# Moving the low parts of MoE 1's 32 weight tiles from VectorE to GpSimd in an attention + two-MoE kernel

## The chip, the core and the metric

The kernel runs on one core of one Trainium2 chip. The metric is the device time of one execution in microseconds (us), the lower the better. The kernel before was timed three times: 968.51, 968.61 and 970.44 us, median 968.61 us.

## The reference: what is computed

Attention with a memory term over B = 4, H = 8, S = 576, D = 64, then two dense feed-forward layers over the 2304 tokens (512 wide, 2048 inner). Cut to what matters:

```python
def _attn_ref(q, k, v, M_prev, z_prev, beta):
    a = softmax(causal(q @ k.T / sqrt(D)))
    mem_out = (phi(q) @ M_prev) / (phi(q) @ z_prev + 1e-6)
    g = sigmoid(beta)
    return g * mem_out + (1 - g) * (a @ v)

def _moe_ref(x, w_in, w_out):      # MoE 1
    h = x @ w_in
    return (h * sigmoid(h)) @ w_out

def _moe2_ref(x, w_in, w_out):     # MoE 2
    h = x @ w_in
    return elu(h) @ w_out

def reference(...):
    return _moe2_ref(_moe_ref(_attn_ref(...)))
```

The weights arrive as 64-bit floats (two 32-bit words each). The kernel rebuilds a 32-bit float from the two words.

## The kernel before, in words

**High and low parts.** TensorE multiplies at its fast rate in a shortened float type (`F32R`). To keep accuracy every operand of the MoE matmuls is held as two tiles: a high part (the value rounded to `F32R`) and a low part (value minus high part). A product is then three matmuls: high x high, high x low, low x high. `split2` (line 474) makes both parts: ScalarE copies the value into the high tile (`nc.scalar.copy`, shown as ACT CAST), and VectorE subtracts it from the value (`sub`, shown as DVE TENSOR_TENSOR).

**The weight stream of MoE 1.** `w_stream` (line 548) brings in 32 weight tiles, f = 0..15 for each of `w_in` (c = 0) and `w_out` (c = 1), in the order (0,0), (0,1), (1,0), ... Each arrives by one DMA of 512 KB into a staging tile. The staging tiles are four slots (`LEND` = 4) in the homes of the last four weight tiles, `w0_14`, `w1_14`, `w0_15`, `w1_15`; the last two tiles pass through two slots called `raw`. `w_value` (line 530) rebuilds the float: ScalarE scales the upper word (ACT ACTIVATE w<-w), VectorE shifts the lower word (TENSOR_SCALAR) and combines the words with two SCALAR_TENSOR_TENSORs. Then `w_split` (line 543) calls `split2`: the high part goes to columns 512 to 1023 of the tile's home, the low part to columns 0 to 511. When both have read the staging slot, the next DMA may fill it. That DMA sits in SyncE's one in-order queue, together with the loads of attention (`q`, `k`, `vr`, `qm`, `zb`, `diag`).

**What runs beside it.** The attention of 20 tasks (scores, mask and maximum on VectorE, exp on ScalarE, scaling, transposes on TensorE, product with V) runs in the first 280 us or so. Into it are woven the first two token blocks of MoE 1 (`moe1_block`, line 611): they use tiles f = 0..7 for both blocks, then tiles f = 8..15 for both. So the weights are wanted one after the other while attention runs. The other MoE 1 blocks and all of MoE 2 follow; MoE 2's weights use the same `w_value`, but their own calls of `split2`.

**GpSimd** does little: a few memsets and masks at the start, and 16 `MEMSET a` of 64x128 (one for each b-part of attention) which wait until TensorE has read the old contents of the five `a` buffers.

**What sets the order.** Nothing is issued in the order of the code. Class `Plan` records every operation, gives it a cost (`cost`, line 239 on) and a lag between engines (`lag`, line 277), and `order` (line 288) runs a list scheduler forwards and backwards 24 times; the best plan fixes each engine's instruction order. A cost counts in that plan only: 602 ns for a 512-column VectorE `tensor_tensor`, and for GpSimd `n / 1.2 + 40` ns (line 268), n being the columns. The planner gives each engine its own time: work on one never makes another slower.

The lines that the change touches:

```python
            return n / 1.2 + 40                    # cost of a GpSimd operation, ns

    def split2(hi, lo, src):
        nc.scalar.copy(hi, src)
        sub(lo, src, f32(hi))

    def w_split(f, c, v):
        t = w_tile(f, c)
        split2(t[:, 512:1024], t[:, 0:512], f32(v))
        (win, wout)[c][f] = t
```

Of the kernel before, what the change touches and what calls it, by code (L numbers as in the profile page):

```python
# [14 lines left out]
ALU = mybir.AluOpType  # L15
# [4 lines left out]
HP = 2000  # L20
OFF = 200
NORM = '3'
XHP = 1000
HOOK = 4
AHEAD = 4
# [132 lines left out]
class Plan:  # L158
# [82 lines left out]
    @staticmethod  # L241
    def cost(op, fn, args, kw, ins, outs, together):
        def cols(v):
            n = 1
            for m in v.shape[1:]:
                n *= m
            return n

        if op.eng == "PE":
            if fn == "transpose":  # L250
                return max(ins[0].shape[0] / 1.2, 0.84 * cols(ins[0]))
            n, m, once = cols(kw["rhs"]), cols(kw["lhsT"]), kw["rhs"].dtype != F32
            if together > 1:
                return n / (2.4 if together > 4 and kw["lhsT"].shape == (64, 64) else 1.2)
            return max(n / (2.4 if once else 0.6) + (13.5 if once else 3.0), 0.84 * m * (1 if once else 2))
        if op.eng == "DMA":
            v = outs[0] if isinstance(outs[0], View) else ins[0]
            n = 4
            for m in v.shape:
                n *= m  # L260
            return max(430.0, n / 280.0)
        n = cols(outs[0])
        psum = any(v.tile.space == "psum" for v in ins)
        if op.eng == "ACT":
            c = n / 1.2 + (51 if psum else 93) + (186 if kw.get("accum_out") is not None else 0)
            return c + (93 if isinstance(kw.get("scale"), View) else 0)
        if op.eng == "POOL":
            return n / 1.2 + 40
        if fn == "tensor_reduce":
            n = cols(ins[0])  # L270
        fast = fn in ("tensor_scalar", "tensor_copy") and not psum
        ptr = any(isinstance(kw.get(k), View) for k in ("scalar1", "scalar2")) or (
            fn == "scalar_tensor_tensor" and isinstance(kw["scalar"], View))
        return 69 + (60 if ptr else 0) + n / (1.92 if fast else 0.96)
# [125 lines left out]
def attention_moe_moe_kernel(  # L400
# [15 lines left out]
    nc = Plan(tc.nc)  # L416
# [21 lines left out]
    def f32(ap):  # L438
        return ap.bitcast(F32)
# [27 lines left out]
    def sub(o, a, b):  # L467
        nc.vector.tensor_tensor(out=o, in0=a, in1=b, op=ALU.subtract)

    def split(t, src):  # L470

        split2(t[:, 0], t[:, 1], src)

    def split2(hi, lo, src):
        nc.scalar.copy(hi, src)
        sub(lo, src, f32(hi))

    ident = new(at, [128, 128], F32, "ident")
    mask = new(at, [128, 704], BF16, "mask")
# [4 lines left out]
        out=ident[:], in_=ident[:], pattern=[[-1, 128]], compare_op=ALU.is_equal,  # L484
# [3 lines left out]
    for p0, rows, c0, n in ((0, 128, 384, 128), (0, 64, 640, 64), (64, 64, 640, 64)):  # L488
        tri = mask[p0:p0 + rows, c0:c0 + n]
        nc.gpsimd.affine_select(  # L490
            out=tri, in_=tri, pattern=[[-1, n]], compare_op=ALU.is_ge, fill=-1e30, base=0, channel_multiplier=1,
# [48 lines left out]
    def w_tile(f, c, dtype=F32R):  # L540
        return new(wp, [128, 1024], dtype, f"w{c}_{f}")

    def w_split(f, c, v):
        t = w_tile(f, c)
        split2(t[:, 512:1024], t[:, 0:512], f32(v))
        (win, wout)[c][f] = t

    def w_stream(srcs, ahead):

        todo = [(f, c) for f in range(NF) for c in range(2)]  # L550
        n = len(todo)
        raws = {}

        def fetch(k):
            if k < n:
                f, c = todo[k]
                i = n - LEND + k % LEND if k < n - LEND else n - 2 + k % 2
                raws[k] = w_load(srcs[c], f, c, w_tile(*todo[i], I32) if k < n - 2 else new(at, [128, 1024], I32, "raw"))

        for k in range(ahead):  # L560
            fetch(k)
        yield
        for k, (f, c) in enumerate(todo):
            raw = raws.pop(k)
            w_value(raw)
            w_split(f, c, raw[:, 0:512])
            if k + ahead < n - 2:
                fetch(k + ahead)
            yield
            if k == n - 3:  # L570
                fetch(n - 2)
                fetch(n - 1)
                yield
# [155 lines left out]
    def soft(task, nms):  # L729
# [48 lines left out]
        for nm, e, off, n, c, m in tiles:  # L778
            if nm in NORM:
                nc.scalar.activation(e[:, off:off + n], e[:, off:off + n], AF.Copy, scale=mx[:, c:c + 1])  # L780
# [87 lines left out]
    def av_end(task, r, av, n):  # L868
        b, p, rg = task
        m = pr_t[task]["m"]  # L870
        mm(av[:, :n], m[:].rearrange("p a d -> p (a d)"), pt_t[task, r][:, :n], False, True)
        xt = pt_t.pop((task, r))
        if (b, r) in early:
            home = x_home((b, r))[p]
            x = [home[:, i].rearrange("p (a n) -> p a n", a=2) for i in range(2)]
            o = av[:, 0:256 if r == "A" else 384].rearrange("p (a n) -> p a n", a=2)[:, :, 0:128]
            split2(x[0], x[1], o)
            if r == "B":
                nc.scalar.copy(xt[:, 0:64], av[:, 128:192])
                nc.sync.dma_start(xd[b, r][p][:, 128:192], xt[:, 0:64])  # L880
        else:
            nc.scalar.copy(xt[:, :n], av[:, :n])
            nc.sync.dma_start(xd[b, r][p], xt[:, :n])
        if p == NP - 1:
            x_done.add((b, r))
# [279 lines left out]
    def x3_load(blks, first=False):  # L1165
        res = []
        for u in range(2):
            raw = new(mp, [128, 4, 256], F32, "stg", 2)[:].rearrange("p a n -> p (a n)")
            raw = raw[:, 0:NT].rearrange("p (k n) -> p k n", k=2)
            x3_part(raw, blks, 0, u, first)  # L1170
            res.append(raw)
        return res

    def x3_split(blks, raws, first=False):

        a, b = raws
        f = {n: form(n, HT) for n in (1, 2, 6, 5, 7, 3, 4)}
        c, d = f32(f[2][:, 1]), f32(f[3][:, 1])
        split(f[1], a)
        x3_part(c, blks, 1, 0, first)  # L1180
        x3_part(d, blks, 1, 1, first)
        nc.scalar.copy(f[2][:, 0], c)
        sub(a, b, a)
        split(f[5], a)
        sub(a, d, a)
        sub(b, b, d)
        split(f[6], a)
        split(f[7], b)
        nc.scalar.copy(f[3][:, 0], d)
        sub(f[3][:, 1], d, f32(f[3][:, 0]))  # L1190
        sub(a, c, a)
        sub(f[2][:, 1], c, f32(f[2][:, 0]))
        split(f[4], a)
        return f
# [135 lines left out]
    def w2_steps(n, end):  # L1330

        for _ in range(n):
            if made[0] < 9 * end:
                made[0] += 1
                next(w2, None)
# [50 lines left out]
    def moe1_seven(blks, i, wnext=None):  # L1386

        wide = len(blks) == 3
        with nc.ahead(XHP):
            if wide:  # L1390
# [40 lines left out]
    w2_steps(99, 2)  # L1431
    with nc.ahead(XHP):
        xn = x3_split(blocks2[0], x3_load(blocks2[0]))
    for v in range(len(visits)):
# [3 lines left out]
        def mid():  # L1438
            if more:
                with nc.ahead(XHP):  # L1440
                    xw[0] = x3_load(blocks2[visits[v + 1][0]])
# [10 lines left out]
        if more:  # L1452
            with nc.ahead(XHP):
                xn = x3_split(blocks2[visits[v + 1][0]], xw[0])
# [55 lines left out]
```

## Time and profile before

| | before |
|---|---|
| median of three runs | 968.61 us |
| profiled execution | 969.0 us, of it the span 967.1 us from the first to the last instruction |
| granted TensorE clock | 1.000 of full speed |
| busy in the span: TensorE matmul | 951.3 us (98%) |
| VectorE | 725.7 us (75%) |
| ScalarE | 604.2 us (62%) |
| GpSimd | 5.9 us (1%) |

How to read it: the shares are means over very different stages. VectorE at 75% of the span is filled to 98% between 80 and 240 us, and half empty later; TensorE at 98% has nearly all of its idle time in the first 80 us. So the views that count are those by stretch of time, and the waits within one stretch. In the views a line such as `TENSOR_TENSOR w<-w,w ... x13 | 8.8, 680` means 13 such instructions, 8.8 us busy together, 680 ns of duration each. Almost all instructions carry line L201, a helper's, so groups are told apart by engine, operation and tile names.

### The profile page before, as it was taken

The page shows a single profiled execution, that of the slowest core. Times are in us where ns is not written, and L with a number is a line of the kernel's source. Part 1 is how long each engine was busy: PE and PEld are TensorE (multiplying, and loading weights), DVE is VectorE, ACT ScalarE, POOL GpSimd, SP SyncE. Part 2 cuts the span into 40 slices and gives each one's busy share as a digit, 9 for nine tenths or more (in the row PEclk, how much of TensorE's full clock was granted, in tenths as well). Part 3 has the DMA queues.
Part 4 walks back from the last instruction along what each step waited for, and adds up shares of the span by engine and source line. Part 5 has one row for each costly group of instructions (what it writes and reads, how often), then busy time and mean ns, then how long its engine had stood idle before and what let it go on. Part 6 is the DMA issues. An engine that isn't in the chain of part 4 may idle for free.

```text
span 967.1 us, 16218 instructions
## 1 busy us (share of the span) xinstructions
PE 951.3 (98%) x5862; PEld 824.6 (85%) x5862; DVE 725.7 (75%) x1629; ACT 604.2 (62%) x1292; POOL 5.9 (1%) x29
## 2 busy tenths in 40 slices
PE   8889999999999999999999999999999999999998
PEld 5467778777789989998999999898989989898987
DVE  7999999999859748765665578888898466548544
ACT  7998999999957456555545466555565344334321
POOL 1000000000000000000000000000000000000000
PEclk9999999999999999999999999999999999999999
DMA  7775456554321012334644435142421014003003
GB/s 212 243 208 178 128 150 197 162 165 139 90 82 35 1 44 93 140 122 148 207 152 131 154 119 163 55 142 77 142 88 44 1 34 120 1 17 116 32 0 109
DMA packets 101951, 107.36 MB, mean 111 GB/s; under 512 B 13040, under 2 KB 80624, under 8 KB 101872
## 3 DMA queue, kind: packets, MB, share of 16 engines
q1 hardware_dynamic: 101584, 106.07, 34.8%
q8 instruction: 46, 0.75, 0.3%
q14 instruction: 33, 0.27, 0.1%
q10 hardware_dynamic: 288, 0.26, 0.1%
HBM read 80.61 MB, written 25.69 MB: 110 GB/s over the span
## 4 chain that ended last, share of the span: by engine, by line
PE 90%; DVE 6%; ACT 2%; DMA 1%; issue 1%; SPq 0%; POOL 0%; DVEq 0%; ACTq 0%; POOLq 0%
PE b L201 49%; PE acc L201 17%; PE av L201 13%; PE h L201 11%; DVE w L201 2%; DVE x L201 1%; DVE eA L201 1%; DVE e L201 1%; ACT e L201 1%; DMA g<-xdB 1%; DVE qm L201 0%; DVE g L201 0%; ACT a L201 0%; DVE nm L201 0%; ACT L201 0%
## 5 line engine op out<-in xcount | busy, mean ns | idle before, releaser
L201 PE MATMUL b<-x,w 128*128 128x384 f32 (+1 forms) x1440 | 263.9, 325 | 0.1
L201 PEld LDWEIGHTS b<-x,w 128*128 128x128 f32 x1440 | 244.2, 188 | 10.8 <-ACT h L201 0.6
L201 ACT COPY x<-b 128x384 f32<-128x384 f32 (+2 forms) x144 | 67.3, 469 | 170.7 <-PE b L201 167.7
L201 DVE TENSOR_TENSOR h<-x,b 128x384 f32<-128x384 f32 (+1 forms) x128 | 66.1, 519 | 115.9 <-PE b L201 100.1
L201 PE MATMUL acc<-g,w 128*128 128x256 f32 (+1 forms) x720 | 146.1, 328 | 2.0 <-DVE g L201 1.1
L201 PEld LDWEIGHTS acc<-g,w 128*128 128x128 f32 x720 | 108.5, 190 | 15.8 <-issue 4.2
L201 PE MATMUL b<-x,g 128*128 128x256 f32 (+1 forms) x552 | 87.6, 301 | 0.0
L201 DVE SCALAR_TENSOR_TENSOR w<-w 128x512 int32<-128x512 int32 x124 | 84.1, 687 | 1.9
L201 PEld LDWEIGHTS b<-x,g 128*128 128x128 f32 x552 | 82.4, 189 | 3.2
L201 PE MATMUL acc<-w,g 128*128 128x512 f32 x288 | 81.0, 390 | 0.0
L201 PE MATMUL b<-w,g 128*128 128x512 f32 x288 | 74.8, 391 | 0.0
L201 ACT ACTIVATE g<-h 128x768 f32<-128x768 f32 x48 | 40.7, 848 | 48.3 <-DVE h L201 47.4
L201 ACT COPY a<-b 128x384 f32<-128x384 f32 (+2 forms) x160 | 62.6, 436 | 1.9 <-PE b L201 1.3
L201 ACT ACTIVATE e<-e,sm 128x512 f32<-128x512 f32 (+2 forms) x88 | 61.4, 718 | 2.9 <-DVE sm L201 2.7
L201 PEld LDWEIGHTS b<-w,g 128*128 128x128 f32 x288 | 53.9, 188 | 10.5
L201 PEld LDWEIGHTS acc<-w,g 128*128 128x128 f32 x288 | 53.7, 188 | 7.7
L201 DVE TENSOR_TENSOR g<-h,g 128x512 fp32r<-128x512 f32 (+1 forms) x48 | 37.4, 779 | 25.3 <-ACT g L201 25.1
L201 PE MATMUL b<-k,q 64*128 64x384 f32 (+5 forms) x368 | 55.1, 450 | 0.3
L201 ACT CAST g<-g 128x768 fp32r<-128x768 f32 x48 | 40.1, 836 | 17.1 <-DVE g L201 11.6
L201 PE MATMUL av<-a,vr 128*64 128x320 f32 (+4 forms) x448 | 50.3, 364 | 0.2 <-DVE x L201 0.2
L201 ACT CAST w<-w 128x512 fp32r<-128x512 f32 (+1 forms) x62 | 36.7, 597 | 19.9 <-DVE w L201 15.5
L201 PEld LDWEIGHTS av<-a,vr 128*64 128x64 f32 x448 | 29.3, 136 | 23.1 <-issue 2.1
(140 smaller groups left out, 1655.7 us busy)
## 6 DMA issues: line engine op xcount, KB each, us to landing
w<-in_moe_w_in SPq DMA_DIRECT2D x31, 512.0 KB, 4.0
w<-in_moe_w_out SPq DMA_DIRECT2D x31, 512.0 KB, 4.0
w1s<-g SPq DMA_DIRECT2D x32, 256.0 KB, 2.0
g<-w1s SPq DMA_DIRECT2D x32, 256.0 KB, 3.8
k<-in_kT SPq DMA_DIRECT2D x16, 288.0 KB, 4.2
qm<-in_qn SPq DMA_DIRECT2D x32, 128.0 KB, 3.0
vr<-in_vn SPq DMA_DIRECT2D x16, 256.0 KB, 3.3
q<-in_qT SPq DMA_DIRECT2D x12, 288.0 KB, 3.2
```

The source lines that it names most:

```text
L201: r = getattr(issue, fn)(*[a.make() if isinstance(a, View) else a for a in args], **{k: v.make() if isinstance(v, View) else v for k, v in ...
```

## The change

GpSimd does the subtraction in `split2` for all 32 weight tiles of MoE 1 (2f + c runs from 0 to 31, `LOW` is 32). The planner's cost of every GpSimd operation becomes `n * 1.6 + 150` ns, 969 ns for 512 columns. MoE 2's weights, and all splits of activations, stay on VectorE.

```diff
+LOW = 32
...
         if op.eng == "POOL":
-            return n / 1.2 + 40
+            return n * 1.6 + 150
...
-    def split2(hi, lo, src):
+    def split2(hi, lo, src, eng=None):
         nc.scalar.copy(hi, src)
-        sub(lo, src, f32(hi))
+        (eng or nc.vector).tensor_tensor(out=lo, in0=src, in1=f32(hi), op=ALU.subtract)
...
-        split2(t[:, 512:1024], t[:, 0:512], f32(v))
+        split2(t[:, 512:1024], t[:, 0:512], f32(v), nc.gpsimd if 2 * f + c < LOW else None)
```

Since the planner sees other engines and costs, it writes a new order for all engines. Three places of it follow. (In the rows `w0_2_0_775` is the home of tile f = 2 of `w_in`, `w1_..` is `w_out`, `w0_14_1_..` a staging slot; `sm`, `e`, `qm`, `em`, `nm` are attention's softmax and memory tiles, `t` and `g` MoE 1's activations.)

First, VectorE around the first activation of MoE 1, `t_0`, in the order before:

```order
L201 TENSOR_SCALAR w0_15_1_737<-w0_15_1_737 128x512 [waits DMAHW5_49]
L201 TENSOR_TENSOR qm_5_548<-qm_5_548,nm_5_739 128x384 [waits DVE_49]
L201 SCALAR_TENSOR_TENSOR w1_14_1_674<-w1_14_1_674 128x512 [waits Activation_49]
L201 SCALAR_TENSOR_TENSOR w0_15_1_737<-w0_15_1_737 128x512 [waits DVE_49,Activation_49]
L201 SCALAR_TENSOR_TENSOR qm_6_719<-em_6_788,qm_6_719 128x384 [waits DMAHW6_49,DMAHW4_49,Activation_49]
L201 TENSOR_TENSOR w0_2_0_775<-w0_14_1_576,w0_2_0_775 128x512
L201 SCALAR_TENSOR_TENSOR w0_15_1_737<-w0_15_1_737 128x512 [waits DVE_49]
L201 TENSOR_TENSOR em_6_788<-qm_6_719,zb_6_760 128x384 [waits DMAHW7_49,DVE_49]
L201 SCALAR_TENSOR_TENSOR w1_14_1_674<-w1_14_1_674 128x512
L201 SCALAR_TENSOR_TENSOR t_0_743<-t_0_743,h_1_479 128x512
L201 TENSOR_TENSOR w0_3_0_866<-w0_15_1_737,w0_3_0_866 128x512 [waits Activation_49]
```

and in the order of the change:

```order
L202 ISA e31_1_729,sm23_1_708<-b2_8_689,mask_0_101 128x512 [waits PE_49]
L202 ISA sm23_1_708 128x1
L202 SCALAR_TENSOR_TENSOR t_0_694<-t_0_694,h_1_481 128x512 [waits Activation_49]
L202 TENSOR_SCALAR e40_1_583<-e40_1_583,sm44_0_577 128x576
L202 SCALAR_TENSOR_TENSOR w1_14_1_614<-w1_14_1_614 128x512 [waits DVE_49]
L202 TENSOR_SCALAR w1_15_1_670<-w1_15_1_670 128x512 [waits DMAHW4_49,Pool_49]
L202 SCALAR_TENSOR_TENSOR w1_14_1_614<-w1_14_1_614 128x512 [waits DVE_49]
L202 SCALAR_TENSOR_TENSOR sm23_1_708<-sm23_1_708,og_0_180 128x4 [waits Activation_49]
L202 RECIPROCAL sm23_1_708<-sm23_1_708 128x4 [waits DVE_49]
L202 SCALAR_TENSOR_TENSOR w1_15_1_670<-w1_15_1_670 128x512
```

The subtractions (TENSOR_TENSOR w..) are gone from VectorE, `t_0` comes 29 rows earlier in its order (row 142, before row 171), and weight steps now wait for GpSimd (Pool).

Second, GpSimd after its opening memsets and masks, before:

```order
L201 AFFINE_SELECT mask_0_101<-mask_0_101 64x64 [waits Pool_49]
L201 MEMSET a_11_579 64x128 [waits PE_49,Activation_49]
L201 MEMSET a_15_762 64x128 [waits PE_49,Activation_49]
L201 MEMSET a_19_955 64x128 [waits PE_49,Activation_49,Pool_49]
L201 MEMSET a_23_1266 64x128 [waits PE_49,Activation_49,Pool_49]
```

and of the change:

```order
L202 AFFINE_SELECT mask_0_101<-mask_0_101 64x64 [waits Pool_49]
L202 TENSOR_TENSOR w0_0_0_462<-w0_14_0_154,w0_0_0_462 128x512 [waits DMAHW7_49,Activation_49,Pool_49]
L202 TENSOR_TENSOR w0_1_0_542<-w0_15_0_330,w0_1_0_542 128x512 [waits DMAHW7_49,Activation_49]
L202 TENSOR_TENSOR w1_0_0_569<-w1_14_0_207,w1_0_0_569 128x512 [waits DMAHW5_49,Activation_49]
L202 MEMSET a_11_622 64x128 [waits PE_49]
L202 TENSOR_TENSOR w1_1_0_620<-w1_15_0_433,w1_1_0_620 128x512 [waits DMAHW6_49,Activation_49]
L202 TENSOR_TENSOR w0_2_0_691<-w0_14_1_514,w0_2_0_691 128x512 [waits DMAHW0_49,Activation_49]
L202 TENSOR_TENSOR w0_3_0_705<-w0_15_1_587,w0_3_0_705 128x512 [waits DMAHW7_49,Activation_49]
```

All 32 subtractions stand on GpSimd, with memsets that wait for TensorE between them.

Third, SyncE's queue where the staging slots are filled for the second time, before:

```order
L201 DMA w_14_1_576<-in_moe_w_in 128x4x256 [waits DMAHW0_49,DVE_49,Activation_49]
L201 DMA q_602<-in_qT 128x320 [waits DMAHW1_49,PE_49]
L201 DMA k_612<-in_kT 128x576 [waits DMAHW2_49]
L201 DMA zb_627<-in_z_prev 128x128 [waits DMAHW3_49,DVE_49]
L201 DMA vr_632<-in_vn 128x4x128 [waits DMAHW4_49,PE_49]
```

and of the change:

```order
L202 DMA w_14_1_514<-in_moe_w_in 128x4x256 [waits DMAHW0_49,Pool_49]
L202 DMA qm_535<-in_qn 128x2x128 [waits DMAHW1_49,DVE_49,PE_49]
L202 DMA qm_535<-in_qn 128x128 [waits DMAHW2_49]
L202 DMA diag_0_127<-in_M_prev 64x64 [waits DMAHW3_49]
L202 DMA diag_0_127<-in_M_prev 64x64 [waits DMAHW4_49]
```

The weight load now waits for GpSimd's subtraction, not VectorE's, and attention's loads stand behind it as they did.

## Rows read from the trace of the kernel before

**Rows 1.** Windows: length; PE, PEld, DVE, ACT, POOL busy (count); clock; DMA share; GB/s.

```profile
0.00:20.00 20.00, 15.97 (x138) 11.74 (x140) 14.61 (x76) 14.48 (x50) 2.44 (x13) 1.00 0.71 214
20.00:80.00 60.00, 52.92 (x370) 36.49 (x371) 59.61 (x164) 53.47 (x131) 0.85 (x4) 1.00 0.72 217
80.00:240.00 160.00, 159.96 (x1276) 123.81 (x1276) 156.71 (x535) 155.17 (x433) 1.79 (x9) 1.00 0.52 157
240.00:280.00 40.00, 40.00 (x328) 31.10 (x324) 29.79 (x104) 36.21 (x99) 0.84 (x3) 1.00 0.27 82
280.00:320.00 40.00, 39.12 (x284) 36.69 (x281) 34.64 (x69) 23.73 (x44) 0.00 (x0) 1.00 0.19 58
320.00:600.00 280.00, 279.86 (x1667) 256.77 (x1666) 184.09 (x321) 153.99 (x274) 0.00 (x0) 1.00 0.38 126
```

**Rows 2.** Instruction groups of VectorE, 0 to 80 us, the subtraction.

```profile
L201 DVE TENSOR_TENSOR w<-w,w 128x512 fp32r<-128x512 f32 x13 | 8.8, 680 | 0.0
```

**Rows 3.** The same view, 80 to 240 us.

```profile
L201 DVE TENSOR_TENSOR w<-w,w 128x512 fp32r<-128x512 f32 x17 | 11.6, 684 | 0.0
...
L201 DVE TENSOR_TENSOR w<-raw,w 128x512 fp32r<-128x512 f32 x2 | 1.4, 688 | 0.0
```

**Rows 4.** Timeline of VectorE: start, duration, instruction.

```profile
71.28 0.69 DVE L201 TENSOR_TENSOR w<-w,w 128x512 fp32r<-128x512 f32 x1
71.88 0.69 DVE L201 SCALAR_TENSOR_TENSOR w<-w 128x512 int32<-128x512 int32 x1
72.48 0.42 DVE L201 TENSOR_SCALAR w<-w 128x512 int32<-128x512 int32 x1
72.82 0.69 DVE L201 SCALAR_TENSOR_TENSOR w<-w 128x512 int32<-128x512 int32 x1
```

**Rows 5.** Waits, 0 to 300 us: who waited for weight tiles.

```profile
PEld h L201 <- DVE w L201: 1.8, 2, 1.2
...
PE h L201 <- DVE w L201: 1.2, 2, 0.8
```

**Rows 6.** Instruction groups of GpSimd, whole span.

```profile
L201 POOL MEMSET a<- 64x128 f32 x16 | 3.5, 217 | 265.4 <-PE av L201 232.9 <-ACT t L201 17.2 <-ACT pt L201 15.4
...
L201 POOL TENSOR_SCALAR_AFFINE_SELECT mask<-mask 64x64 bf16<-64x64 bf16 x2 | 0.5, 236 | 0.1
L201 POOL TENSOR_SCALAR_AFFINE_SELECT ident<-ident 128x128 f32<-128x128 f32 x1 | 0.3, 295 | 0.0
```

**Rows 7.** Instruction groups of VectorE, 27 to 231 us: the largest beside the subtraction.

```profile
L201 DVE SCALAR_TENSOR_TENSOR w<-w 128x512 int32<-128x512 int32 x58 | 39.5, 685 | 0.3
...
L201 DVE CUSTOM_DVE_ANT_0 e<-b,mask 128x384 f32<-128x384 f32 x38 | 19.9, 548 | 0.0
L201 DVE CUSTOM_DVE_ANT_0 e<-b,mask 128x512 f32<-128x512 f32 x24 | 15.7, 684 | 0.3 <-PE b L201 0.2
L201 DVE TENSOR_SCALAR w<-w 128x512 int32<-128x512 int32 x28 | 11.7, 420 | 0.0
L201 DVE TENSOR_TENSOR g<-t,g 128x512 fp32r<-128x512 f32 x12 | 8.2, 684 | 0.0
L201 DVE SCALAR_TENSOR_TENSOR t<-t,h 128x512 f32<-128x512 f32 x12 | 8.2, 680 | 0.1
L201 DVE CUSTOM_DVE_ANT_0 eA<-b,mask 128x256 f32<-128x256 f32 x18 | 7.5, 417 | 0.0
L201 DVE TENSOR_TENSOR em<-qm,zb 128x384 f32<-128x384 f32 x13 | 7.2, 553 | 0.2
L201 DVE SCALAR_TENSOR_TENSOR qm<-em,qm 128x384 f32<-128x384 f32 x13 | 7.2, 552 | 0.2 <-ACT qm L201 0.2
```

**Rows 8.** Instruction groups of ScalarE, 0 to 80 us, weights.

```profile
L201 ACT ACTIVATE w<-w 128x512 f32<-128x512 f32 x15 | 10.3, 687 | 0.0
L201 ACT CAST w<-w 128x512 fp32r<-128x512 f32 x14 | 8.7, 618 | 4.1 <-DVE sm L201 2.4 <-DVE w L201 1.6
```

**Rows 9.** DMA issues: KB each, median us to landing.

```profile
w<-in_moe_w_in SPq DMA_DIRECT2D x31, 512.0 KB, 4.0
```

## The prediction, made before the changed kernel ran

> **What bounds the kernel now.** I read the windows first [rows 1], because a mean over 967 us hides three stages. From 80 to 280 us TensorE is busy for 159.96 of 160 and 40.00 of 40 us: no other engine can give anything back there, whatever it is spared. From 320 to 600 us it is 279.86 of 280. TensorE stands idle at the start only: 4.0 us of the first 20, before any weight has come, and 60 - 52.92 = 7.1 us between 20 and 80 us. In that second stretch VectorE is busy 59.61 of 60 us: there VectorE is the bound, and TensorE waits for what it makes. From 80 to 240 us both are full (VectorE 156.71 of 160, 3.3 us to spare); from 240 to 280 VectorE has 10.2 us to spare.
>
> Then I looked for what VectorE does there. The subtraction that moves is 13 of its instructions before 80 us [rows 2] and 17 + 2 between 80 and 240 us [rows 3]: all 32. The timeline gives the true price of one [rows 4]: a subtraction starts at 71.28 and the next instruction at 71.88, so one costs 0.60 us of the engine, not the 0.68 of its duration, since neighbours overlap. Last, the waits [rows 5]: TensorE itself and its weight loads waited for VectorE's weight tiles only four times, 1.2 + 1.8 = 3.0 us. The other idle time went to other VectorE and ScalarE results, which are late because VectorE's queue is full.
>
> **The change, part by part.**
>
> *VectorE is relieved* of 32 x 0.60 = 19.2 us, 13 x 0.60 = 7.8 us of it before 80 us. Of this at most the 7.1 us of idle TensorE between 20 and 80 us can reach the end. The 19 later ones (11.4 us) meet a full TensorE and are worth nothing by themselves; what is late next there is TensorE's own work.
>
> *GpSimd gets 32 subtractions* of 512 columns. No row has one. Nearest are its masks [rows 6]: 295 ns for 128 columns and 236 for 64, so 59 ns for 64 columns or 0.92 ns per column, and 236 + 448 x 0.92 = 650 ns for 512 columns with one input. A subtraction has two inputs; if these follow each other it takes twice that, 1.3 us. I take 1.1 us, nearer to the upper end, as two inputs are what it has. Over 32 that is 35 us in 220: GpSimd is never full. [...]
>
> *Does GpSimd slow VectorE?* This decides. No row answers it: GpSimd's only reading instructions, the masks, run before VectorE begins, and the 16 memsets only write [rows 6]. The lower bound is nothing, the upper the whole length of a subtraction, 1.1 us each. What rows do show is that VectorE's work around the weights is of two kinds. One reads two SBUF tiles at once (SCALAR_TENSOR_TENSOR w, g, em, qm) or one at almost twice the rate (TENSOR_SCALAR w: 0.34 us from start to start for 512 columns, where the others take 0.60 [rows 4]). The other reads PSUM and one SBUF tile (the masked scores e and eA, and t). In the largest groups the first kind has 39.5 + 11.7 + 8.2 + 7.2 + 7.2 = 73.8 us, the second 19.9 + 15.7 + 8.2 + 7.5 = 51.3 us [rows 7], so 59% is of the first kind. I take it that the first kind and a GpSimd instruction that reads SBUF exclude each other, and that the second kind goes on. Then a GpSimd subtraction costs VectorE 0.59 x 1.1 = 0.65 us on average, against 0.60 saved: 0.05 us more each, 0.7 us for the 13 early ones. For the 19 later ones it is 1.0 us, which the 3.3 us to spare hide; without that cover they would add it in full.
>
> [...]
>
> *The low part is ready later.* From the end of ScalarE's high part, VectorE needed 0.68 us. GpSimd needs 1.1 us, and before it up to 0.60 us until VectorE's running instruction is through, 0.2 on average (0.59 of half of it): 0.6 us later in all. The planner, which counts 969 ns and no exclusion, has pulled `t_0` ahead from row 171 to row 142 and asks for the tiles sooner. The first 16 tiles are used as they come; I let each of the four waits of TensorE [rows 5] grow by 0.6 us: 2.4 us. Bounds: nothing, if the new order leaves room, and 16 x 0.6 = 9.6 us, if every one of the 16 stalls TensorE.
>
> *Queues.* On GpSimd, 16 memsets that wait for TensorE now have subtractions behind them. Their waits were the engine's whole idle time before (232.9 us for TensorE), but in the new order each stands where its buffer is nearly free, so I cost it at nothing; one that comes late delays every low part behind it. On SyncE a weight load waits for GpSimd and has attention's loads behind it. A slot's turn is the load 4.0 us [rows 9], ScalarE 0.69 and 0.62 [rows 8], VectorE 0.34 + 0.60 + 0.60 [rows 4] and the subtraction, 7.5 us in all. With 13 tiles in 60 us and four slots there are 18 us for it, so 0.6 us more is hidden by 11 us of slack. ScalarE's work is unchanged. MoE 2 is unchanged.
>
> *Sum*, against the profiled execution's 969.0 us: + 0.7 (VectorE early) + 2.4 (late low parts) = + 3.1, so 972.1 us; the median of the runs shown is 0.4 us below that execution, so some 972 us is predicted. A measurement of this kernel can tell about 0.2%, 1.9 us, from no change.
>
> **The rivals.**
>
> 1. *GpSimd works beside VectorE without touching it* (faster). For it: nothing in the trace shows a conflict, and the memsets did no visible harm. Against it: 59% of VectorE's work reads more than one stream, and GpSimd reads the same memory. VectorE then gains 7.8 us before 80 us; TensorE's idle time there falls by at most 7.1. Less some 1 us for later low parts that is 6 us: 963 us. It decides as soon as a GpSimd subtraction costs VectorE less than about 0.3 us. Chance 0.32.
> 2. *The exchange is even* (the same). The exclusion costs VectorE what it saves, and the planner's new order hides the later low parts. This needs only the 2.4 us to be under 1.9. 969 us. Chance 0.18.
> 3. *The exclusion costs its upper bound* (much slower). If a subtraction takes 1.3 us and nearly always holds VectorE for 1.2 us, each costs 0.6 us net: 13 x 0.6 = 7.8 us before 80 us, and 19 x 0.6 - 3.3 = 8.1 us after, as TensorE has no slack there: 985 us. For it: the weights' steps are the largest group [rows 7], so the next VectorE instruction is often of the first kind. Against it: masked scores come in runs of four to eight. Chance 0.12.
>
> That the change does not do what it says is excluded: the new order has the 32 subtractions on GpSimd and none on VectorE.
>
> **How the numbers follow.** The forecast, some 3 us slower (971 to 978), has 0.38. So faster by over 0.2% 0.32, within 0.2% 0.18, slower 0.50. For 8 in 10 the range takes in most of the first rival, which ends at 962 (969.0 less the whole 7.1), and reaches up through the forecast's bounds (0.7 + 9.6 = 10.3 us, 979) to 982, short of the third rival's middle. Since both signs hold much of the chance: the likeliest case's own range is 969 to 979.
>
> **What would show it right or wrong.** GpSimd's group TENSOR_TENSOR w should have 32 instructions of about 1.1 us, with longer ones where they wait. VectorE's instructions that overlap them should last longer than their 0.69 us, by up to 1 us, while masked scores keep theirs; VectorE's busy time would then fall by far less than 19 us. TensorE's idle time between 20 and 80 us should be 7 us or a little more; if it is 1 or 2, the first rival holds. In 80 to 240 us TensorE should stay nearly full; an idle time of several us there, released by POOL w, means the third rival or a low part that comes too late. The forecast is wrong if VectorE's instructions keep their durations beside GpSimd's.

## The result, and the profile after

After: 982.57 us, median of four runs (981.89 to 983.05); before, with a fourth run beside it: 969.23 us (968.51 to 970.44). The ratio is 1.0136, 95% interval [1.0118, 1.0153]: 13.3 us slower. The forecast had the sign (some 3 us slower, 972.0) but a quarter of the size, and the result lies 0.6 us above the range's upper end of 982.

Windows of the kernel after, in the columns of [rows 1]:

```profile
0.00:20.00 20.00, 15.59 (x130) 12.05 (x131) 13.64 (x70) 13.76 (x46) 2.45 (x13) 1.00 0.74 209
20.00:80.00 60.00, 47.31 (x326) 32.89 (x325) 58.81 (x145) 48.71 (x118) 17.84 (x15) 0.94 0.64 196
80.00:240.00 160.00, 155.73 (x1232) 119.29 (x1232) 153.69 (x488) 151.42 (x417) 27.71 (x29) 1.00 0.53 157
240.00:280.00 40.00, 39.88 (x312) 30.24 (x310) 34.97 (x124) 36.34 (x106) 1.91 (x4) 1.00 0.35 103
```

Between 20 and 80 us TensorE now idles 12.7 us (7.1 before), between 80 and 240 us 4.3 us (0.04 before). VectorE, which gave 32 subtractions away, is as full as it was: 58.81 and 153.69 against 59.61 and 156.71, and it carries work past 240 us (34.97 against 29.79). From 320 us on TensorE's idle time is the same (3.8 us in both). Over the whole span TensorE idles 26.2 us (15.8 before) and is busy for 954.3 us (951.3): of the 13.4 us by which the span grew, 10.4 are waiting and 3.0 are matmuls that took longer. Why VectorE is still full, its groups say (whole span):

```profile
L202 DVE SCALAR_TENSOR_TENSOR w<-w 128x512 int32<-128x512 int32 x124 | 86.2, 702 | 2.6
...
L202 DVE TENSOR_SCALAR w<-w 128x512 int32<-128x512 int32 x62 | 30.5, 496 | 0.0
...
L202 DVE CUSTOM_DVE_ANT_0 e<-b,mask 128x384 f32<-128x384 f32 x48 | 24.9, 550 | 0.0
...
L202 DVE TENSOR_TENSOR qm<-qm,nm 128x384 f32<-128x384 f32 x16 | 10.7, 668 | 0.3
L202 DVE TENSOR_TENSOR em<-qm,zb 128x384 f32<-128x384 f32 x16 | 10.5, 654 | 0.4
```

The shift of the weights' steps takes 496 ns where it took 420, and em 654 where it took 553 [rows 7], though only some of each met a GpSimd subtraction; the masked scores stay at 550 (548). The groups of GpSimd:

```profile
L202 POOL TENSOR_TENSOR w<-w,w 128x512 fp32r<-128x512 f32 x30 | 42.4, 1416 | 157.9 <-ACT w L202 135.3 <-DMA vr<-in_vn 22.5
...
L202 POOL TENSOR_TENSOR w<-raw,w 128x512 fp32r<-128x512 f32 x2 | 2.6, 1294 | 6.7 <-ACT w L202 6.7
```

The shortest of the 32 took 1.27 us, the longest 2.36. One meeting in the timeline, GpSimd's two rows first and then VectorE's:

```profile
43.53 1.32 POOL L202 TENSOR_TENSOR w<-w,w 128x512 fp32r<-128x512 f32 x1 [3.92 <-ACT w L202]
46.65 1.28 POOL L202 TENSOR_TENSOR w<-w,w 128x512 fp32r<-128x512 f32 x1 [1.80 <-ACT w L202]
```

```profile
43.64 1.63 DVE L202 TENSOR_TENSOR qm<-qm,nm 128x384 f32<-128x384 f32 x1
45.19 0.68 DVE L202 SCALAR_TENSOR_TENSOR w<-w 128x512 int32<-128x512 int32 x1
...
46.60 0.55 DVE L202 CUSTOM_DVE_ANT_0 e<-b,mask 128x384 f32<-128x384 f32 x1
...
47.08 0.68 DVE L202 CUSTOM_DVE_ANT_0 e<-b,mask 128x512 f32<-128x512 f32 x1
```

The sum qm (two SBUF inputs) begins 0.11 us after a subtraction and takes 1.63 us, usually 0.55; it ends 0.42 us after the subtraction does, as if it had gone on only then. The masked scores at 46.60 and 47.08 run beside the next subtraction with their usual 0.55 and 0.68. Over the whole trace I took each VectorE instruction that overlaps a GpSimd subtraction, less the median of the same instruction in before: 19.5 us in all, 0.61 us for each of the 32. That is the prediction's exclusion (0.65), and just what one subtraction had cost VectorE (0.60).

So VectorE's load is even, and yet 13.3 us are lost. What TensorE waited for from 20 to 240 us (waits; us, times, longest):

```profile
PE b L202 <- DVE sm L202: 9.0, 5, 3.1
PE b L202 <- DVE smA L202: 1.8, 2, 1.0
...
PE h L202 <- POOL w L202: 0.4, 1, 0.4
```

Not for the low parts (0.4 us), but for transposes of scores that VectorE scales late. In the chain of waits VectorE's share rose from 6% to 11%, TensorE's fell from 90% to 78%.

### The profile page after: what moved, and what is told of

The parts are those of the page before. It is cut to its first block, busy times and chain, and to the rows that moved or that the text cites. A ratio compares the mean times of both kernels' runs of the same rounds, so it can differ in the third digit from the quotient of the medians.

```text
span 980.5 us, 16283 instructions
## 1 busy us (share of the span) xinstructions
PE 954.3 (97%) x5862; PEld 826.7 (84%) x5862; DVE 732.9 (75%) x1597; ACT 605.6 (62%) x1292; POOL 50.1 (5%) x61
## 4 chain that ended last, share of the span: by engine, by line
PE 78%; DVE 11%; ACT 5%; issue 3%; DMA 2%; POOL 0%; SPq 0%; DVEq 0%; ACTq 0%; POOLq 0%
PE b L202 44%; PE acc L202 15%; PE av L202 10%; PE h L202 9%; DVE w L202 3%; DVE e L202 2%; ACT e L202 2%; DVE nm L202 1%; ACT a L202 1%; DVE qm L202 1%; DVE x L202 1%; DVE eA L202 1%; DVE g L202 1%; ACT w L202 1%; DVE t L202 1%
## 5 line engine op out<-in xcount | busy, mean ns | idle before, releaser
L202 DVE SCALAR_TENSOR_TENSOR w<-w 128x512 int32<-128x512 int32 x124 | 86.2, 702 | 2.6
L202 ACT ACTIVATE g<-h 128x768 f32<-128x768 f32 x48 | 40.7, 848 | 48.3 <-DVE h L202 47.4
L202 PE MATMUL b<-ident,e 128*128 128x128 f32 x304 | 49.4, 279 | 9.0 <-DVE sm L202 4.7
L202 ACT CAST g<-g 128x768 fp32r<-128x768 f32 x48 | 40.1, 836 | 17.2 <-DVE g L202 11.6
```

Of the source, the lines that this page charges most:

```text
L202: r = getattr(issue, fn)(*[a.make() if isinstance(a, View) else a for a in args], **{k: v.make() if isinstance(v, View) else v for k, v in ...
```

## The experiments

Three causes were possible after the traces: the hold (GpSimd's reads stop VectorE's instructions at bad moments), the lateness of the low parts (L), and the new order (O, which counts on a VectorE that is free). A fourth, a lower granted clock of TensorE, is looked at in the traces of these runs. Each run gives its ratio to before on the same chip and, where it bears on the question, the time by which VectorE's instructions were lengthened, worked out as above.

**First question: GpSimd, or the new order?** The change does both. Two runs do one each. The old order, each subtraction merely issued by GpSimd (the planner takes it for VectorE's):

```
-        split2(t[:, 512:1024], t[:, 0:512], f32(v))
+        hi, lo, v = t[:, 512:1024], t[:, 0:512], f32(v)
+        nc.scalar.copy(hi, v)
+        nc.add("vector", [("tensor_tensor", (), dict(out=lo, in0=v, in1=f32(hi), op=ALU.subtract))], "gpsimd")
```

> Order of the kernel before on every engine; only the 32 subtractions are issued by GpSimd, each at its old place. Measured in the changed kernel: VectorE's instructions that overlap GpSimd's subtractions are 19.5 us longer in all, 0.61 us for each, against 0.60 us saved. Theory O (the new order asks VectorE for work sooner than it can come, since the planner believes in the relief): with the old order nearly all of the loss goes, 969 to 973 us. Theory L (the low parts come 0.6 to 1.2 us later and TensorE waits for them wherever they are made by GpSimd): 977 to 983 us, about as slow as the changed kernel, with TensorE waiting for POOL w.

Measured 976.94 us, 1.0073 [1.0056, 1.0090]: 6.9 us slower, half of the change's loss (13.3). VectorE's instructions were lengthened by 20.3 us. L falls: from 20 to 240 us TensorE waited 0.5 us for a low part, and the low part ended 1.37 us after the high part (2.40 before), so sooner.

The new order, executed by VectorE: the same line with "gpsimd" and "vector" exchanged, in the kernel after.

> Order of the changed kernel on every engine; only the 32 subtractions are issued by VectorE, at the places that the plan had given GpSimd. VectorE then has 32 x 0.60 = 19 us more than the plan believes, and no exclusion. Theory O: as slow as the changed kernel, 980 to 986 us, since exclusion costs VectorE the same 0.6 us for each. Theory L: back to some 969 to 973 us, since the low parts are made in 0.69 us again.

Measured 979.68 us, 1.0100 [1.0085, 1.0115]: 9.7 us slower, with no subtraction on GpSimd. TensorE's longest wait of the kernel after stands there as well (timeline; first of the kernel after, then of this run):

```profile
35.06 0.91 PE L202 MATMUL b<-ident,e 128*128 128x128 f32 x4 [3.09 <-DVE sm L202]
```

```profile
34.18 0.69 PE L202 MATMUL b<-ident,e 128*128 128x128 f32 x2 [2.61 <-DVE sm L202]
```

My reading is that the new order puts other VectorE work ahead of these scores, since by its account VectorE has time; when VectorE has not, TensorE waits, whoever makes the low parts. So O has a share, but not the whole. Both halves cost, and together (13.3) less than their sum (16.6).

**Second question: what holds VectorE, and what does it cost?** Four runs in the order of before leave VectorE its subtractions and add one instruction behind each of the 32 weight tiles' decoding, on a half of the slot that is dead by then. The GpSimd one that reads:

```
+    def beside(op, raw):
+        first, dead = op.run, raw[:, 512:1024].bitcast(F32)
+        def run():
+            r, d = first(), dead.make()
+            tc.nc.gpsimd.tensor_tensor(out=d, in0=d, in1=d, op=ALU.subtract)
+            return r
+        op.run = run
...
             w_value(raw)
+            beside(nc.ops[-1], raw)
```

> Kernel before, with its order; after each of the 32 weight values GpSimd also subtracts the dead half of the staging slot from itself, 512 columns, two SBUF inputs, the result used by nobody. Nothing is taken from VectorE. If a GpSimd instruction that reads SBUF and a VectorE instruction with two SBUF inputs exclude each other, VectorE loses 32 x about 0.6 = 19 us in the first 240 us, little of which finds a gap: 980 to 990 us, with TENSOR_TENSOR, SCALAR_TENSOR_TENSOR and TENSOR_SCALAR up to 1.2 us longer and the masked scores unchanged. If there is no exclusion: 969 to 971 us.

Measured 987.21 us, 1.0177 [1.0162, 1.0193]: 17.2 us slower, with VectorE's instructions lengthened by 17.8 us. The order is that of before and the low parts are VectorE's, so neither O nor L can explain it: the hold is real, and the time lost is nearly as long as the hold (how much of it is waiting, and how much the clock, follows below).

In the next run two `gpsimd.memset(d, 0.0)` take the subtraction's place, writes of the same size and about the same time (571 and 548 ns on average, against 1207 for the subtraction):

> As the run with the extra subtraction, but GpSimd writes the dead half twice (two memsets of 512 columns, some 0.55 us each, no input). If only reading counts against VectorE's two-input instructions: 969 to 974 us, at most TENSOR_SCALAR longer. If any GpSimd access to SBUF holds VectorE: 978 us or more, two-input instructions longer as well.

Measured 971.28 us, 1.0013 [1.0004, 1.0022]: 1.3 us slower; VectorE lengthened by 2.5 us, nearly all of it in one-input instructions at nearly double rate (TENSOR_SCALAR, 0.34 us from start to start for 512 columns where the others take 0.60 [rows 4]; eA of 256 columns took 383 ns on average, 346 before). So it is the reading. Is it the two inputs? `gpsimd.tensor_copy(out=d, in_=d)`:

> Like the run with the extra reads, but the extra GpSimd instruction is a copy of the dead half onto itself: one input read in place of two. Nothing is left out. Theory S (every read by GpSimd holds VectorE's two-input instructions): they are lengthened as by the subtraction, in proportion to the copy's own length, so 977 to 988 us. Rival T (only a GpSimd instruction with two inputs holds them): lengthening in the double-rate copies alone, as with the writes, 970.5 to 974 us.

Measured 977.48 us, 1.0085 [1.0069, 1.0101]: 8.2 us slower, lengthened by 7.4 us. T falls: one input that is read is enough. Theory S holds, though not in proportion to the copy's length: 0.23 us for each copy (777 ns on average), 0.56 for each subtraction (1207 ns). The rows side by side, GpSimd's group (whole span) and two of VectorE's (27 to 245 us), of the extra subtraction, the extra copy and the writes in turn (for the writes the first memset of each pair; the second has a line of its own):

```profile
L553 POOL TENSOR_TENSOR w<-w 128x512 f32<-128x512 f32 x30 | 36.2, 1207 | 180.5 <-DVE w L201 63.7 <-ACT pt L201 24.6 <-ACT a L201 23.5
...
L201 DVE CUSTOM_DVE_ANT_0 e<-b,mask 128x384 f32<-128x384 f32 x38 | 19.9, 549 | 1.0 <-PE b L201 1.0
...
L201 DVE TENSOR_TENSOR g<-t,g 128x512 fp32r<-128x512 f32 x11 | 10.9, 991 | 0.0
```

```profile
L553 POOL COPY w<-w 128x512 f32<-128x512 f32 x30 | 23.2, 777 | 183.0 <-DVE w L201 58.0 <-ACT pt L201 32.3 <-ACT em L201 24.1
...
L201 DVE CUSTOM_DVE_ANT_0 e<-b,mask 128x384 f32<-128x384 f32 x40 | 20.8, 546 | 0.0
...
L201 DVE TENSOR_TENSOR g<-t,g 128x512 fp32r<-128x512 f32 x12 | 9.8, 819 | 0.0
```

```profile
L553 POOL MEMSET w<- 128x512 f32 x30 | 17.1, 571 | 167.9 <-DVE w L201 32.4 <-ACT a L201 31.1 <-ACT pt L201 28.0
...
L201 DVE TENSOR_TENSOR g<-t,g 128x512 fp32r<-128x512 f32 x12 | 8.2, 686 | 0.0
```

The product g, with two SBUF inputs, takes 991, 819 and 686 ns (684 in [rows 7]); the masked scores, with one input in PSUM, 549 and 546 (548). So GpSimd's reads lengthened VectorE's instructions by 17.8 and 7.4 us, its writes by 2.5 us.

Last of the four, the extra subtraction on VectorE itself (`tc.nc.vector` for `tc.nc.gpsimd`):

> The twin of the run with the extra reads (before + 17.2 us): the same 64 extra subtractions of the slot's dead half from itself, at the same place, now issued by VectorE itself. Nothing is left out. If each takes the 0.60 us of a subtraction of before, that is 38 us of plain VectorE work where the holds had come to 17.8 us. Theory K (VectorE and TensorE are both full up to 240 us, so a microsecond put on VectorE, as a hold or as work, is lost whole): 1.0 us for each us of work that lies before 240 us; half of the 64 lie there in before, so +17 to +21 us, 986 to 991 us, with about 0.95 us of time for each us added, the same price as the hold's (17.2 for 17.8). Rival G (a hold is dearer than work, since it hits instructions that the plan put first): a price of 0.6 or less for each us added, under 982 us.

Measured 991.01 us, 1.0225 [1.0208, 1.0242]: 21.8 us slower. The expectation miscounted: the extras are 32, not 64, all before 260 us, 22.1 us by their durations (691 to 693 ns) and 32 x 0.61 = 19.5 by their steps. The price is then 1.0 to 1.1 us for each us added, the hold's 17.2 / 17.8 = 0.97. By these totals a hold is about as dear as work, as theory K has it, and rival G falls. In the chain of waits VectorE has 22% (6% before).

Part of both prices is TensorE's granted clock. The windows of the two profiled runs, the extra subtraction on GpSimd first, then on VectorE:

```profile
20.00:80.00 60.00, 50.99 (x329) 34.41 (x328) 58.66 (x153) 50.76 (x125) 14.30 (x14) 0.91 0.66 201
80.00:240.00 160.00, 153.26 (x1183) 117.81 (x1181) 157.23 (x481) 145.29 (x395) 25.53 (x29) 0.98 0.48 148
```

```profile
20.00:80.00 60.00, 49.29 (x317) 33.48 (x318) 59.23 (x158) 50.39 (x124) 0.79 (x4) 0.94 0.65 199
80.00:240.00 160.00, 151.57 (x1166) 115.46 (x1164) 157.50 (x498) 142.86 (x390) 1.69 (x8) 1.00 0.48 147
```

Both runs have before's matmuls in before's order, so each matmul can be set against its twin. Those that ran while the clock was at the lower of its two levels (0.50 of full speed, the other 1.00) took 7.3 us longer in the first run and 2.8 us longer in the second. Of the 19.4 and 21.7 us by which the two spans grew, 12.1 and 18.9 are left: some 0.7 us for each us of hold, and 0.9 to 1.0 for each us of work. So the equal price of hold and work is in part the clock's doing; why the clock fell more in the first run was not tested.

**Third question: what is the relief worth?** Each subtraction is replaced by two GpSimd memsets of the low half, so VectorE is relieved and not held by reads. In the order of the change, then in the order of before:

```
-        split2(t[:, 512:1024], t[:, 0:512], f32(v), nc.gpsimd if 2 * f + c < LOW else None)
+        hi, lo, v = t[:, 512:1024], t[:, 0:512], f32(v)
+        nc.scalar.copy(hi, v)
+        op = nc.gpsimd.tensor_tensor(out=lo, in0=v, in1=f32(hi), op=ALU.subtract)
+        def run():
+            d = f32(lo).make()
+            tc.nc.gpsimd.memset(d, 0.0)
+            return tc.nc.gpsimd.memset(d, 0.0)
+        op.run = run
```

> The order of the change word for word, but in the place of each subtraction GpSimd writes zeros over the low half twice (two memsets of 512 columns, 1.05 us, no reads). The low parts of MoE 1's weights are therefore zero: that part of the computation is left out, the matmuls are all there. VectorE is relieved of 32 x 0.60 us and, by the run with added writes (+1.3 us), hardly held. Theory O: the order's belief is now true, so it must gain: 963 to 968 us, by up to the 7.1 us that TensorE idled between 20 and 80 us. Theory P: the order itself is bad, so it stays above before: 972 to 977 us. Theory H alone (only the holds matter, not the order): 964 to 969 us as well, so this run speaks between O and H together and P.

Measured 970.09 us, 1.0000 [0.9990, 1.0009]: no change. P's 972 is missed, and so are the 968 and 969 us at most that O and H wanted. The same order lost 13.3 us with the subtractions in it, so it does no harm where VectorE is really relieved.

> The order of before word for word, with each subtraction of MoE 1 replaced by two GpSimd memsets of the low half (writes, no reads), so VectorE is relieved and not held. The low parts are zero: that part of the computation is left out, the matmuls are all there. Theory K: TensorE had 0.04 us of idle time between 80 and 240 us, so relief can only earn what TensorE idled before 80 us, 7.1 us at most, and the run with the new order and no reads earned nothing: 966 to 970 us. Rival R (the relief is worth its 19.2 us less the 1 to 3 us of the writes, and it was the re-planned order that ate it): 952 to 962 us.

Measured 969.58 us, 1.0000 [0.9991, 1.0009]: no change; rival R falls. The windows of this last run, and what VectorE waited for from 20 to 240 us (its largest rows), with those of before under them:

```profile
20.00:80.00 60.00, 52.57 (x374) 37.03 (x371) 57.03 (x161) 55.51 (x137) 17.79 (x34) 1.00 0.74 227
80.00:240.00 160.00, 159.95 (x1277) 123.62 (x1277) 148.03 (x509) 153.11 (x429) 18.74 (x41) 1.00 0.51 156
```

```profile
DVE t L201 <- ACT t L201: 2.6, 2, 1.9
DVE sm L201 <- ACT e L201: 2.5, 5, 0.9
DVE e L201 <- PE b L201: 2.5, 4, 0.7
DVE em L201 <- DMA zb<-in_z_prev: 1.0, 1, 1.0
```

```profile
DVE em L201 <- DMA zb<-in_z_prev: 0.6, 1, 0.6
DVE qm L201 <- ACT qm L201: 0.3, 2, 0.2
DVE e L201 <- PE b L201: 0.2, 1, 0.2
```

VectorE is freed of 11 us (57.03 + 148.03 against 59.61 + 156.71; the memsets still lengthened its fast one-input instructions by 5.4 us, so the relief is 19.2 - 5.4 = 13.8 us net). The memsets don't read the staging slot either, so it can come free sooner, which could only help. Yet TensorE is as busy as it was: 52.57 against 52.92, 159.95 against 159.96. The freed time has become VectorE's own waiting for ScalarE, TensorE and a transfer: 11.6 us in nine kinds where it was 1.1 in three. VectorE and TensorE sit at a kink: a microsecond more on VectorE costs about one (0.7 in the run with the hold, if the clock's part is left out), a microsecond less is worth nothing.

**Fourth question: does a planner that knows repair it?** The planner gets GpSimd's true price and the hold:

```
-            return n * 1.6 + 150
+            return 1280.0 if fn == "tensor_tensor" else n / 1.2 + 40
...
+            if e == "POOL" and o.cost == 1280.0:
+                free["DVE"] = max(free["DVE"], t) + 610.0
```

> GpSimd does all 32 subtractions, as in the change, but the planner is told what they cost: 1.28 us on GpSimd, and 0.61 us on VectorE from the moment each starts (the hold that the traces of the change and of the first run show); the memsets keep their old price. Theory O (the change loses because its order counts on a relief of VectorE by 19.2 us that does not come): the order is made for the load that VectorE has, so 970 to 973 us, within 0.3% of before. Theory P (the order of before is a lucky one, and any other order of this program is some us worse, whatever it counts on): 975 to 982 us. Theory H (the holds fall on urgent VectorE instructions at moments that no plan chose): 975 to 978 us, since the moments are still not the plan's.

Measured 978.37 us, 1.0085 [1.0070, 1.0100]: 8.5 us slower; VectorE lengthened by 19.2 us. Theory O falls as the whole cause: an order that counts the hold loses about what the old order loses. In the profiled runs TensorE idles 4.4 us longer than before here and 4.2 us longer in the old order with GpSimd; the rest is longer matmuls, here at a granted clock of 0.89 from 20 to 80 us.

The control, with the changed price line alone on the kernel before:

> Before with nothing changed but the planner's price of GpSimd's few memsets and masks (1.6 ns a column + 150 ns in place of 0.83 ns + 40 ns), the price line of the change. VectorE does every subtraction, and the planner counts it so; the order that comes out differs from that of before nearly everywhere in the first third. Theory O: an order made for the true load, so 968.5 to 972 us. Theory P: 974 to 980 us, like the order of the change executed by VectorE (979.7 us).

Measured 969.26 us, 0.9991 [0.9982, 1.0001]: theory P falls. A different order that counts VectorE's load rightly costs nothing.

Last, the old order with GpSimd held back to VectorE's place, by a dependence of each subtraction on the VectorE instruction that stood ahead of it:

> The order of before with the subtractions on GpSimd, as in the first run (976.9 us), but each of them also waits for the VectorE instruction that stood just ahead of it in before, so it starts where VectorE would have made it and no sooner. Nothing is left out. Theory H (in the first run GpSimd starts at once when the high part is ready, about a microsecond ahead of the plan's place, and holds instructions that the plan had put first): 970.5 to 973.5 us, since the hold now replaces the subtraction at its own place, 0.61 for 0.60 us. Rival, lumps: what costs is that one or two VectorE instructions are held for up to 1.2 us wherever it happens: 975 to 979 us, as in the first run. Rival L (lateness of the low parts): 979 us and more, since the low parts come still later, with TensorE's waits for GpSimd's w tile above 3 us in the sum (0.5 us in the first run).

Measured 978.55 us, 1.0086 [1.0069, 1.0102]: 8.7 us slower, in the range of the rival with the lumps; H falls in the form stated. The run is no clean test: VectorE was still lengthened by 18.0 us, and TensorE now did wait for low parts (20 to 240 us):

```profile
PE h L201 <- POOL w L201: 2.9, 3, 1.8
...
PE acc L201 <- POOL w L201: 0.7, 2, 0.3
```

**What stays open** is the size of the loss in the old order with GpSimd: 6.9 us, where hold and relief by steps are 20.3 - 19.2 = +1.1. Against the relieved run the hold adds 20.3 - 5.4 = 14.9 us to VectorE. VectorE's idle time between 20 and 240 us is 14.9 us there and 7.2 us here, so 7.8 us were absorbed, and some 7 were not. The same matmuls run in the same order there, so each can be set against its twin in before: 3.8 us late at 100 us, 3.8 at 170, 6.4 at 190, 6.2 at 200, and 6.6 to 7.0 from 230 us on. Of these, 1.1 us are matmuls that took longer at the lower clock. One of the steps, from the timeline of that run:

```profile
183.50 0.20 POOL L201 MEMSET a<- 64x128 f32 x1 [8.53 <-PE av L201]
...
183.66 1.27 POOL L201 TENSOR_TENSOR w<-w,w 128x512 fp32r<-128x512 f32 x1
...
183.87 1.49 DVE L201 SCALAR_TENSOR_TENSOR qm<-em,qm 128x384 f32<-128x384 f32 x1
...
185.30 1.27 POOL L201 TENSOR_TENSOR w<-w,w 128x512 fp32r<-128x512 f32 x1 [0.37 <-ACT w L201]
...
185.75 1.24 DVE L201 TENSOR_TENSOR em<-qm,zb 128x384 f32<-128x384 f32 x1
...
186.91 0.34 DVE L201 TENSOR_SCALAR eA<-eA,smA 128x256 f32<-128x256 f32 x1
...
187.31 0.44 PE L201 MATMUL b<-ident,eA 128*128 128x128 f32 x2 [1.09 <-DVE eA L201]
```

A memset that waited 8.53 us for TensorE kept a subtraction behind it, whose high part had been ready 3.4 us before; two then ran almost back to back, held qm by 0.94 and em by 0.69 us, and the scaling behind them came 1.09 us late for TensorE. My reading is that time taken off VectorE can't be stored (it becomes waiting), while time put on it in lumps is lost as soon as TensorE has nothing else. This step shows it once; that it makes up all the 6.9 us was not shown.

## Why the prediction was right or wrong

- **What bounds the kernel.** Right for 80 to 280 us: relief earned nothing there. Wrong for 20 to 80 us: "there VectorE is the bound". VectorE was full there, but with its subtractions gone it got through 161 other instructions in that stretch (151 before), and TensorE's busy time did not move (52.57 against 52.92). What holds TensorE there instead was not settled: its largest waits in the relieved run were still for VectorE (sm 1.6 us, t 1.3 us), and VectorE's for ScalarE. And TensorE's idle time before lay less in the first 80 us than "nearly all": 11.1 of 15.8 us.
- **VectorE is relieved, at most 7.1 us reach the end.** The ceiling held, but the value is nothing, in either order.
- **GpSimd's subtraction, 1.1 us (0.65 to 1.3).** Too low: 1.27 us at the shortest, 1.42 on average, which is above the upper bound. The one-input 650 ns worked out from the masks was good: the copy took 0.61 us at the shortest, 0.78 on average. No run shows the 1.1 us that the sum uses, my choice between 0.65 and 1.3; the runs show 1.27 to 2.36 us in its place.
- **The exclusion, 0.65 us each.** Right in size (0.61) and in kind (the masked scores untouched, 550 ns for 548), but the size is partly luck: it was 0.59 of 1.1 us, and what was measured is 0.43 of 1.42. That the two exclude each other was my assumption, which no run had shown by then; the extra subtractions, copies and writes then showed 17.8, 7.4 and 2.5 us of lengthening.
- **The set-off, "0.05 us more each", + 0.7 us early and 1.0 us hidden late.** This is the step that failed. It subtracts a relief of 0.60 from a hold of 0.65 as if both were worth the same. The runs showed a hold of 17.8 us at 17.2 us of time (in the profiled run 7.3 of its 19.4 through the clock) and a relief of 19.2 us (13.8 net) at nothing. With both together in the old order, where the set-off has + 0.7 us, it came to + 6.9: relief gave back a part of the hold, by my reading only where VectorE was late just then.
- **The low part is ready later, + 2.4 us.** Wrong. TensorE waited 0.4 us for GpSimd's tiles. From the end of ScalarE's high part to the end of the low part it took 1.39 us in the median, 2.40 before: GpSimd starts when the high part is there, where VectorE had made the low part as filler when its queue came to it.
- **Queues at nothing.** Not right for GpSimd's own: the step at 183 us came from a memset. SyncE's waits for weight tiles up to 90 us changed little (14.1 us for VectorE's before, 15.5 for GpSimd's and 2.1 for VectorE's after), but 6.5 us of waiting for memsets of `a` are new.
- **The new order.** It was used for the low parts alone, "the planner asks for the tiles sooner". What mattered was what it did to VectorE's sequence: counting on a relief that didn't come, it cost 9.7 us with VectorE executing, and takes the kernel from + 6.9 to + 13.3 us. The sum had no term for it.
- **The rivals.** The first falls twice: there is an exclusion, and without it nothing is gained. The second (an even exchange) has the load right and the time wrong. The third comes nearest in time (985), but its price of 0.6 us net per subtraction wasn't found: VectorE's load is even.

## What to carry to other kernels

Before work is moved off a full engine, ask what a microsecond less on it is worth and what a microsecond more costs: where two engines are full together, the first can be nothing and the second most of it or all (here nothing, and 0.7 to 1.1 us), so gain and harm must not be set off against each other. In this kernel work moved from VectorE to GpSimd came back as a hold, since it reads SBUF (17.8 us with the extra subtractions, 2.5 with writes alone): a two-input subtraction of 512 columns saved VectorE 0.60 us and held it for 0.61, in a mix where most of VectorE's work is of the kind that is held (59% in the largest groups of [rows 7]). And when a planner makes the order, a wrong belief about one engine moves everybody's work (9.7 us here with VectorE executing): run the new order with the old executor, and the old order with the new one, to see the two costs apart.

## What was not expected of the hardware

- The holds here were not in proportion to the held instruction: qm of 384 columns lost 1.08 us beside a subtraction of 1.32 us, and the one-input copy of 0.61 us still lengthened g by 135 ns on average (819 against 684).
- A GpSimd subtraction of a tile from itself took 1.04 us at the shortest and 1.21 on average, one of two different tiles 1.27 and 1.42 us. The first writes f32 and the second fp32r; which difference counts was not tried.
- TensorE's granted clock between 20 and 80 us fell to 0.94 after (1.00 in [rows 1]). It was at the lower of its two levels (0.50 of full speed, the other 1.00) from 47.4 to 54.2 us, behind a stretch in which TensorE was busy for 4.66 of 6.90 us, and rose again behind one in which it was busy for 5.91 of 6.80:

```profile
40.50:47.40 6.90, 4.66 (x31) 3.24 (x31) 6.76 (x16) 5.24 (x11) 2.07 (x2) 1.00 0.69 192
47.40:54.20 6.80, 5.91 (x19) 2.87 (x20) 6.41 (x15) 6.69 (x17) 1.88 (x2) 0.50 0.66 204
54.20:61.00 6.80, 6.59 (x55) 5.48 (x52) 6.71 (x21) 6.39 (x18) 1.42 (x2) 1.00 0.62 205
```

The busy time of the same 5862 matmuls grew from 951.3 to 954.3 us. The clock's part in this has a bound, by an estimate: eight k,q matmuls of 384 columns took 3.36 us at the clock of 0.50 and 1.77 us at 1.00 in before; if all that were busy for those 5.91 us would take half at 1.00, they lost 3.0 us, so of the change's 13.3 us at most some 3 are the clock's. It can cost less: the control ran with the same 0.94 from 20 to 80 us, was busy for 951.8 us, and lost nothing.
